# Sparse attention with a feed-forward layer on one core: a causal triangle added by TensorE in place of a select on GpSimd, and another order in the fourth slot

## The chip, the cores and the metric

The kernel runs on one core of a Trainium2 chip. A core has TensorE (PE: matmuls; PEld: its weight loads), VectorE (DVE), ScalarE (ACT), GpSimd (POOL) and SyncE (SP); DMA transfers are issued by SP, ACT and POOL. The metric is the time of one execution on the device in microseconds (us).

## The reference

Two stages follow each other: attention in which each query looks at the best six of 24 chunks of 32 keys, then a feed-forward layer with a squared ReLU.

```python
B, H, S, D = 4, 8, 768, 64          # chunk = 32, top_k = 6
ub = sum(maximum(q * k_min, q * k_max), -1)      # a bound for each query and chunk
ub = where(pos // 32 >= chunk_index, ub, -1e9)
top_chunks = argsort(ub)[..., -6:]
scores = q @ k.T / sqrt(D)
mask = (chunk of key in top_chunks) & (pos_q >= pos_k)
attn = softmax(where(mask, scores, -1e9))
x = (attn @ v)                       # heads side by side: (3072, 512)
out = maximum(x @ w_in, 0) ** 2 @ w_out          # w_in 512 x 2048, w_out 2048 x 512
```

Inputs and output are float32.

## The kernel before

The work is cut into eight half batches (one batch element, 384 of its 768 queries), in the order `ORDER`: first halves of batches 0 and 1, second halves of both, then batches 2 and 3. A half batch has four *slots*, each a pair of heads; there are 32 slots, and `NP` is 4. A first half sees only the keys of its own three tiles of 128.

The steps of a slot `s`:

- `step_T` transposes k and q of the two heads on TensorE (tiles `tk`, `tq`). ACT makes `qr`, the positive and the negative part of q (`relus_T`); DVE finds each chunk's minimum and maximum (`extrema`, L231, L234: `km`, `kbd`); `place` copies k and q into `kq`.
- `step_U` computes the bounds `ub` on TensorE (L372, L376), their eight largest on DVE (L390) and the choices (L392).
- `step_V` transposes the choices on TensorE (L425; L436 from slot 4 on) and copies them into `kq` (L430; L441), below q's 64 rows. There they meet rows that hold -2^24 at each chunk's keys, so that the score matmul itself takes chunks that are not chosen far down.
- `step_E(s, hh, n)` computes transposed scores of head `hh` (keys on partitions, queries along the columns), bank `n` of `BANKS`, on TensorE (L454, tile `ps`, three buffers), and their exponential on ACT (L460, tile `e`). In a first half, bank 0 holds key tile 0 against three query tiles and key tile 2 against one; bank 1 holds key tile 1 against two. After bank 1, one `affine_select` on POOL (L464) puts zeros above the diagonal of the three square tiles.
- `step_F` multiplies `e` with v (L482, tile `po`; a column of ones beside v gives the sum), divides (L491, L492) into `x`.

When a half batch is done, `x_T` transposes its x and `x_copy` moves it to `xT` (L520, L526), and `push` puts its feed-forward pieces into a queue: 16 `ffn_up` (L568, four matmuls each, then ReLU and square) and `ffn_down` (L591). They are taken from the queue one by one between the steps of later slots. `busy(n)` issues `n` dummy matmuls of ident with ident (L674) whose result nobody reads.

All is emitted in an order written out by hand: each engine takes its instructions in program order and waits on the semaphores of what it needs. The tiles `ub`, `qt`, `po` and `idle` (the dummies') share one pool of two buffers, `psA`, in order of their creation. The first four slots have the order of the loop at L708; from slot 4 on the loop at L750 holds. POOL's order in the first 30 us is: the identity, loads of k, q and v, and then, between the selects of slots 0 to 3, further loads (`later`, run by `go`): codes, w_in, v, k, q, w_out.

Of the kernel before, what the change touches and what calls it, by code (L numbers as in the profile page):

```python
# [9 lines left out]
BF16 = mybir.dt.bfloat16  # L10
AX = mybir.AxisListType
ALU = mybir.AluOpType
# [7 lines left out]
OFFSEL = -float(2 ** 24)  # L20


BANKS = (
# [3 lines left out]
)  # L27
# [12 lines left out]
def kernel(  # L40
# [61 lines left out]
    def load_packed(n, g, h0=0, h1=H):  # L102

        nc.gpsimd.dma_start(
            out=packed(n, g)[:, h0:h1],
            in_=rows(n, *ORDER[g], h0, h1).rearrange("h (p j) d -> p h (j d)", j=TP))
# [7 lines left out]
    def load_q0(h):  # L114
        nc.gpsimd.dma_start(
            out=qn0[:, :, h // 2, h % 2, 0:D],
            in_=q[0, h, 0:HB].rearrange("(j p) d -> p j d", p=128))
# [31 lines left out]
        nc.vector.memset(vn[i][:, :, :, D:D + 1], 1.0)  # L149
    ident = consts.tile([128, 128], BF16, tag="ident")  # L150
    make_identity(nc, ident)
    load_packed("k", 0, 4)
    for h in (4, 5):
        load_q0(h)
# [1 line left out]
        load_vt(0, j, 0, H // 2)  # L156
    for h in (6, 7):
        load_q0(h)
    for n in "kq":
        load_packed(n, 1)  # L160
    for j in range(HT):
# [61 lines left out]
    def extrema(s, part=None):  # L223
        b, half, p = slots[s]
        kv = st[s]["k"].rearrange("r (j c e) -> r c j e", j=TP, c=12)
        if part in (None, 0):
            st[s]["km"] = work.tile([128, 2, 12], BF16, tag="km", name="km")
        km = st[s]["km"]
        for w in range(2):
            if part in (None, w):  # L230
                nc.vector.tensor_reduce(km[:, w, :], kv, axis=AX.XY, op=(ALU.min, ALU.max)[w])  # L231
        if part in (0, 1):
            return
        nc.vector.tensor_mul(  # L234
            kbds[b % 2][:, p, :, :, 12 * half:12 * half + 12], hmask,
            km.unsqueeze(2).to_broadcast([128, 2, 2, 12]))
# [54 lines left out]
    def place(s, n, copy, h0=0, h1=2):  # L291
        b, half, p = slots[s]
        for h in range(h0, h1):
            copy(by_token(kqs[b % 2][0:D, p, 2 * half + "kq".index(n), h, :]),  # L294
                 in_order(st[s][n][D * h:D * h + D]))
# [67 lines left out]
    def step_U(s):  # L363
        b, half, p = slots[s]
        st[s]["e"] = [None, None]
        ncs = 12 * (half + 1)
        j0 = 1 - half
        nj = HT - j0
        bank = psA.tile([128, 192], F32, tag="att", name="ub")
        ub = bank[:, 0:2 * nj * ncs].rearrange("p (j h c) -> p j h c", j=nj, h=2)  # L370
        if not half:
            nc.tensor.matmul(  # L372
                bank[:, 0:48], lhsT=ident, rhs=cmask[:, 0:48], start=True, stop=False)
        for j in range(j0, HT):
            for w in range(2):
                nc.tensor.matmul(  # L376
                    ub[:, j - j0], lhsT=st[s]["qr"][:, w, 128 * j:128 * (j + 1)],
                    rhs=kbds[b % 2][:, p, w, :, 0:ncs],
                    start=bool(half) and j == 0 and w == 0,
                    stop=(not half and j == HT - 1 and w == 1))  # L380
        if half:
            diag = bank[:, 12:12 + HT * 52].rearrange("p (j x) -> p j x", j=HT)
            nc.tensor.matmul(  # L383
                diag[:, :, 0:48].rearrange("p j (h c) -> p j h c", h=2)[:, :, :, 0:4],
                lhsT=ident, rhs=cdiag[:, 0:1].to_broadcast([128, HT, 2, 4]),
                start=False, stop=True)
        m8 = work.tile([128, HT, 2, 8], F32, tag="m8", name="m8")
        for j in range(j0, HT):
            for hh in range(2):
                nc.vector.max(out=m8[:, j, hh, :],  # L390
                              in_=ub[:, j - j0, hh, 0:12 * half + 4 * j + 4])
        nc.vector.tensor_tensor(  # L392
            (qn0[:, j0:, p, :, D:D + ncs] if s < NP else
             chosen[s % 2][:, j0:, :, 0:ncs] if s < ON_PE * NP else
             nsel[half][:, s % 2, :, j0:, 1, 0:ncs].rearrange("p h j c -> p j h c")),
            ub, m8[:, j0:, :, TOPK - 1:TOPK].to_broadcast([128, HT - j0, 2, ncs]),
            op=ALU.is_lt)

    def qc(s, h):
        b, half, p = slots[s]  # L400
        return kqs[b % 2][0:KR, p, 2 * half + 1, h, :]
# [16 lines left out]
    def step_V(s):  # L418
        b, half, p = slots[s]
        if s < NP or s == ON_PE * NP:  # L420

            qt = psA.tile([128, 2, HB], BF16, tag="att", name="qt")
            for hh in range(2):
                for j in range(HT):
                    nc.tensor.matmul(  # L425
                        qt[0:KR, hh, 128 * j:128 * (j + 1)],
                        lhsT=qn0[:, j, p, hh, :] if s < NP else
                        nsel[half][:, s % 2, hh, j].rearrange("r n d -> r (n d)")[:, 0:KR],
                        rhs=ident, is_transpose=True, start=True, stop=True)
            nc.vector.tensor_copy(kqs[b % 2][0:KR, p, 2 * half + 1], qt[0:KR])  # L430
            return
        j0 = 1 - half
        c = 128 * j0
        qt = psA.tile([128, HB], BF16, tag="att", name="qt")
        for j in range(j0, HT):
            nc.tensor.matmul(  # L436
                qt[0:2 * CR, 128 * j:128 * (j + 1)],
                lhsT=chosen[s % 2][:, j].rearrange("r h c -> r (h c)"),
                rhs=ident, is_transpose=True, start=True, stop=True)
        for h in range(2):  # L440
            nc.vector.tensor_copy(  # L441
                kqs[b % 2][D:KR, p, 2 * half + 1, h, c:], qt[CR * h:CR * h + CR, c:])

    def step_E(s, hh, n):
        b, half, p = slots[s]
        t = st[s]
        if n == 0:
            t["e"][hh] = work.tile([128, 1920], BF16, tag="e", bufs=4, name="e")
        e = t["e"][hh]
        ps = psS.tile([128, 512], F32, tag="ps", name="ps")  # L450
        lo, hi = 512, 0
        for (at, j, i0, m) in BANKS[half][n]:
            c = 128 * (i0 - HT * half)
            nc.tensor.matmul(  # L454
                ps[:, at:at + 128 * m],
                lhsT=kqs[b % 2][0:KR, p, 2 * (j // HT), hh,
                                128 * (j % HT):128 * (j % HT + 1)],
                rhs=qc(s, hh)[:, c:c + 128 * m], start=True, stop=True)
            lo, hi = min(lo, at), max(hi, at + 128 * m)
        nc.scalar.activation(e[:, 512 * n + lo:512 * n + hi], ps[:, lo:hi], ACT.Exp,  # L460
                             scale=float(scale))
        if n == 1:
            d = e[:, 0:1152].rearrange("p (a c) -> p a c", a=3)[:, :, 0:128]
            nc.gpsimd.affine_select(  # L464
                out=d, in_=d, compare_op=ALU.is_ge, fill=0.0, base=0,
                channel_multiplier=-1, pattern=[[0, 3], [1, 128]])
# [203 lines left out]
    def busy(n, pool=psA, tag="att"):  # L670

        idle = pool.tile([128, 128], F32, tag=tag, name="idle")
        for _ in range(n):
            nc.tensor.matmul(idle, lhsT=ident, rhs=ident, start=True, stop=True)  # L674
# [32 lines left out]
    late = ctx.enter_context(tc.tile_pool(name="late", bufs=2))  # L707
    for s in range(NP):  # L708
        last = s + 1 == NP
        if s:  # L710
            step_E(s, 0, 0)
            if not last:

                step_T(s + 2, F, Y, "k")
                extrema(s + 2, 0)
            step_E(s, 0, 1)
        step_E(s, 1, 0)
        step_U(s + 1)
        busy(6)
        if not last:  # L720
            extrema(s + 2, 1)
            place(s + 1, "k", nc.scalar.copy)
        step_E(s, 1, 1)
        if last:
            x_T(0, 0, F)
            x_copy(0, 0, 0, 2, nc.scalar.copy)
            place(s + 1, "q", nc.scalar.copy)
            place(s + 1, "k", nc.scalar.copy, 1, 2)
        else:
            step_T(s + 2, F, Y, "q")  # L730
            relus_T(s + 2)
        step_V(s + 1)
        if s:
            step_F(s - 1, 0)
            step_F(s - 1, 1)
        if last:
            step_F(s, 0)
            step_F(s, 1)
        else:
            extrema(s + 2, 2)  # L740
            if s + 2 == NP:
                place(s + 2, "k", nc.vector.tensor_copy, 0, 1)
        go(s, 99)
# [181 lines left out]
```

## Time and profile before

| | |
|---|---|
| median of 3 runs | 267.62 us (267.55 to 269.31) |
| the profiled execution | 267.47 us |
| its span, from the first to the last instruction | 265.7 us |
| mean granted TensorE clock | 0.994 of full speed |
| busy: PE, ACT, DVE, POOL | 256.1, 178.0, 163.4, 94.5 us |

A row of the timeline has the start and the length in us, the engine, the line, the operation, out<-in, sizes, how many instructions of the kind were merged (x6), and in brackets how long the engine had been idle before it and what ended that. `idle` in a row's operands is the dummies' tile. A row of the table by stretches has for each engine the busy time and, in brackets, the number of instructions; then PEclk, the granted clock, the mean busy share of the DMA engines, and GB/s. A row of the chain has start, length and what was on the chain.

### The profile page before, as it was taken

To read this page: it belongs to the slowest core of one execution; us is meant where nothing else is said; L and a number is where in the kernel's file an instruction comes from. 1 tells how busy PE (TensorE), PEld (TensorE's weight loads), DVE (VectorE), ACT (ScalarE), POOL (GpSimd) and SP (SyncE) were. 2 spreads that over 40 slices of the span, in tenths; PEclk is the share of its full clock that TensorE was granted. 3 is DMA by queue.
4 is the path that set the end of the run, shared out by engine and by line. 5 is a ranking of instruction groups with operands and counts; after the bars stand their busy time and mean duration, and the time that the engine had idled before them with its cause. 6 is when DMAs were issued, how large, how long until landed. Compare 5 with 4: busy or idle time off the path is not lost.

```text
span 265.7 us, 6574 instructions
## 1 busy us (share of the span) xinstructions
PE 256.1 (96%) x2415; PEld 157.1 (59%) x2415; DVE 163.4 (61%) x618; ACT 178.0 (67%) x399; POOL 94.5 (36%) x141
## 2 busy tenths in 40 slices
PE   7887999999999999999999999999999999999995
PEld 6564566556656566655665566655565566745543
DVE  6895899776987468556875576555863233424421
ACT  5996798588976688845575787934685788614500
POOL 8998446515912425225611544221120111000000
PEclk9998899999999999999999999999999999999999
DMA  7999999999993799999996999996542220111022
GB/s 135 171 185 188 205 217 191 114 178 114 151 169 77 141 154 166 117 181 129 185 153 138 136 142 168 197 87 158 123 99 69 72 44 17 56 42 41 0 81 79
DMA packets 116161, 33.69 MB, mean 127 GB/s; under 512 B 102560, under 2 KB 112576, under 8 KB 116128
## 3 DMA queue, kind: packets, MB, share of 16 engines
q0 software_dynamic: 65200, 13.83, 64.3%
q1 hardware_dynamic: 49984, 19.03, 38.6%
q10 hardware_dynamic: 944, 0.39, 0.6%
q8 instruction: 19, 0.31, 0.5%
q14 instruction: 14, 0.11, 0.1%
HBM read 27.26 MB, written 6.29 MB: 126 GB/s over the span
## 4 chain that ended last, share of the span: by engine, by line
PE 78%; DVE 8%; POOL 5%; ACT 3%; DMA 2%; issue 2%; DVEq 0%; POOLq 0%; ACTq 0%
PE py L591 29%; PE ph L568 27%; PE ps L454 11%; PE po L482 7%; DMA kn<-in_k_dram 2%; DVE km L337 2%; POOL vn L125 2%; POOL e L464 2%; PE ub L376 1%; ACT e L460 1%; PE py L556 1%; DVE km L231 1%; DVE kq L441 1%; DVE h L579 1%; DVE kq L294 1%
## 5 line engine op out<-in xcount | busy, mean ns | idle before, releaser
L460 ACT ACTIVATE e<-ps 128x512 bf16<-128x512 f32 x192 | 96.4, 550 | 19.5 <-PE ps L454 19.2
L568 PE MATMUL ph<-xT,w_in 128*128 128x384 bf16 x512 | 100.1, 328 | 0.1
L591 PE MATMUL py<-w_out,h 128*128 128x512 bf16 x368 | 88.1, 379 | 0.5 <-DVE kq L294 0.3
L464 POOL TENSOR_SCALAR_AFFINE_SELECT e<-e 128x384 bf16<-128x384 bf16 x64 | 34.2, 540 | 131.2 <-ACT e L460 130.3
L579 DVE TENSOR_TENSOR h<-ht 128x384 bf16<-128x384 bf16 x114 | 41.8, 376 | 55.6 <-ACT ht L578 55.0
L578 ACT ACTIVATE ht<-ph 128x384 bf16<-128x384 f32 x114 | 55.5, 500 | 27.0 <-PE ph L568 26.5
L568 PEld LDWEIGHTS <-w_in 128*128 128x128 bf16 x512 | 48.2, 98 | 31.1 <-issue 2.2
L454 PE MATMUL ps<-kq 96*128 96x384 bf16 (+2 forms) x320 | 57.6, 278 | 1.3 <-DVE kq L430 0.9
L591 PEld LDWEIGHTS <-h 128*128 128x128 bf16 x368 | 34.6, 97 | 35.6 <-issue 0.6
L454 PEld LDWEIGHTS <-kq 96*128 96x128 bf16 x320 | 26.4, 97 | 16.2 <-issue 1.7
L482 PEld LDWEIGHTS <-e 128*128 128x128 bf16 x672 | 25.3, 98 | 6.0 <-POOL e L464 2.3
L482 PE MATMUL po<-vn,e 128*128 128x65 bf16 x672 | 27.0, 194 | 1.8 <-POOL e L464 1.5
L597 ACT COPY ob<-py 128x512 f32<-128x512 f32 x18 | 10.6, 586 | 22.6 <-PE py L591 22.3
L390 DVE MAX8 m<-ub 128x8 f32<-128x16 f32 (+4 forms) x160 | 16.1, 166 | 15.4 <-PE ub L383 9.3
L492 DVE TENSOR_TENSOR x<-po,r 128x384 bf16<-128x384 f32 x32 | 17.8, 557 | 1.1
L109 POOL DMA_DIRECT2D kn<-in_k_dram x15 | 13.3, 892 | 0.4 <-issue 0.3
L109 POOL DMA_DIRECT2D qn<-in_q_dram x15 | 13.3, 893 | 0.2
L231 DVE TENSOR_REDUCE km<-tk 128x12 bf16<-128x384 bf16 x24 | 12.5, 551 | 0.9 <-PE tk L268 0.7
L125 POOL DMA_DIRECT2D vn<-in_v_dram x15 | 12.5, 841 | 0.7 <-issue 0.6
L337 DVE TENSOR_TENSOR km<-km 128x384 bf16<-128x384 bf16 (+3 forms) x40 | 11.7, 294 | 1.1
L376 PEld LDWEIGHTS <-qr 128*128 128x128 bf16 x160 | 7.9, 96 | 5.3 <-DVE qr L317 1.7
L376 PE MATMUL ub<-kbd,qr 128*128 128x48 bf16 (+1 forms) x160 | 9.7, 180 | 1.3 <-DVE kbd L234 0.5
(75 smaller groups left out, 188.5 us busy)
## 6 DMA issues: line engine op xcount, KB each, us to landing
out_dram<-ob SPq DMA_DIRECT2D x23, 256.0 KB, 2.7
w_out<-in_moe_w_out_dram POOLq DMA_DIRECT2D x2, 1024.0 KB, 16.8
kn<-in_k_dram POOLq DMA_DIRECT2D x15, 128.0 KB, 5.6
qn<-in_q_dram POOLq DMA_DIRECT2D x15, 128.0 KB, 5.5
kq<-kqT SPq DMA_DIRECT2D x10, 192.0 KB, 4.8
vn<-in_v_dram POOLq DMA_DIRECT2D x4, 384.0 KB, 8.2
vn<-in_v_dram POOLq DMA_DIRECT2D x9, 128.0 KB, 8.1
w_in<-in_moe_w_in_dram POOLq DMA_DIRECT2D x2, 512.0 KB, 8.0
```

The lines of the kernel that those rows point to most:

```text
L109: nc.gpsimd.dma_start(out=nat_of(n, g)[:, DM * j:DM * j + DM].rearrange("p (h d) -> p h d", d=D), in_=rows(n, *ORDER[g], 0, H)[:, 128 * j: ...
L125: nc.gpsimd.dma_start(out=vn[b % 2][:, h0:h1, j, 0:D], in_=v[b, h0:h1, 128 * j:128 * (j + 1)].rearrange("h p d -> p h d"))
L376: nc.tensor.matmul(ub[:, j - j0], lhsT=st[s]["qr"][:, w, 128 * j:128 * (j + 1)], rhs=kbds[b % 2][:, p, w, :, 0:ncs], start=bool(half) and ...
L454: nc.tensor.matmul(ps[:, at:at + 128 * m], lhsT=kqs[b % 2][0:KR, p, 2 * (j // HT), hh, 128 * (j % HT):128 * (j % HT + 1)], rhs=qc(s, hh)[: ...
L460: nc.scalar.activation(e[:, 512 * n + lo:512 * n + hi], ps[:, lo:hi], ACT.Exp, scale=float(scale))
L464: nc.gpsimd.affine_select(out=d, in_=d, compare_op=ALU.is_ge, fill=0.0, base=0, channel_multiplier=-1, pattern=[[0, 3], [1, 128]])
L482: nc.tensor.matmul(po[:, hh, i, :], lhsT=t["e"][hh][:, c:c + 128], rhs=vn[b % 2][:, 2 * p + hh, j, :], start=(j == 0), stop=(j == iq))
L492: nc.vector.tensor_mul(x[:, p].rearrange("p j (h d) -> p h j d", h=2), po[:, :, :, 0:D], r.to_broadcast([128, 2, HT, D]))
L568: nc.tensor.matmul(ph[:, 0:HB], lhsT=w_in[:, ki, 128 * f:128 * (f + 1)], rhs=xT[:, ki, :], start=(ki == 0), stop=(ki == NKI - 1))
L578: nc.scalar.activation(ht, ph[:, 0:HB], ACT.Relu)
L579: nc.vector.tensor_mul(h, ht, ht)
L591: nc.tensor.matmul(py[t], lhsT=h2[hb, f][:, 128 * t:128 * (t + 1)], rhs=w_out[:, f, :], start=(f == 0), stop=(f == NFI - 1))
```

## The change

1. A constant `tri` of 128 x 128 is made at the start: DVE fills it with -2^24, and POOL, after the loads of q for heads 6 and 7, keeps that where the partition is greater than the column and puts zeros elsewhere.
2. In slots 0 to 3, `step_E` adds `tri` to each square tile on the diagonal with a matmul (weights `ident`, 128 columns) behind the scores, in the same bank: two in bank 0 and one in bank 1. The `affine_select` is left out there, and stays for slot 4 and later.
3. In slots 0 to 2 there are three dummies behind the bounds in place of six. In slot 3 the six are left out, and four stand ahead of its scores.
4. In slot 3, slot 2's products (`step_F(s - 1)`) move ahead of slot 4's bounds (`step_U`), and slot 4's choices (`step_V`) move behind slot 3's own products.

```diff
     ident = consts.tile([128, 128], BF16, tag="ident")
     make_identity(nc, ident)
+
+    tri = consts.tile([128, 128], BF16, tag="tri", name="tri")
+    nc.vector.memset(tri, OFFSEL)
     load_packed("k", 0, 4)
...
     for h in (6, 7):
         load_q0(h)
+    nc.gpsimd.affine_select(
+        out=tri, in_=tri, compare_op=ALU.is_ge, fill=0.0, base=-1,
+        channel_multiplier=1, pattern=[[-1, 128]])
     for n in "kq":
         load_packed(n, 1)
...
-                rhs=qc(s, hh)[:, c:c + 128 * m], start=True, stop=True)
+                rhs=qc(s, hh)[:, c:c + 128 * m], start=s >= NP or lo == 512, stop=s >= NP)
             lo, hi = min(lo, at), max(hi, at + 128 * m)
+        if s < NP:
+            for (at, j, i0, m) in BANKS[half][n]:
+                nc.tensor.matmul(
+                    ps[:, at:at + 128], lhsT=ident, rhs=tri, start=False,
+                    stop=at == BANKS[half][n][-1][0])
         nc.scalar.activation(e[:, 512 * n + lo:512 * n + hi], ps[:, lo:hi], ACT.Exp,
                              scale=float(scale))
-        if n == 1:
+        if n == 1 and s >= NP:
             d = e[:, 0:1152].rearrange("p (a c) -> p a c", a=3)[:, :, 0:128]
             nc.gpsimd.affine_select(
...
     for s in range(NP):
         last = s + 1 == NP
+        if last:
+            busy(4)
         if s:
             step_E(s, 0, 0)
...
             step_E(s, 0, 1)
         step_E(s, 1, 0)
+        if last:
+            step_F(s - 1, 0)
+            step_F(s - 1, 1)
         step_U(s + 1)
-        busy(6)
         if not last:
+            busy(3)
             extrema(s + 2, 1)
             place(s + 1, "k", nc.scalar.copy)
         step_E(s, 1, 1)
...
             place(s + 1, "q", nc.scalar.copy)
             place(s + 1, "k", nc.scalar.copy, 1, 2)
+            step_F(s, 0)
+            step_F(s, 1)
+            step_V(s + 1)
         else:
             step_T(s + 2, F, Y, "q")
             relus_T(s + 2)
-        step_V(s + 1)
-        if s:
-            step_F(s - 1, 0)
-            step_F(s - 1, 1)
-        if last:
-            step_F(s, 0)
-            step_F(s, 1)
-        else:
+            step_V(s + 1)
+            if s:
+                step_F(s - 1, 0)
+                step_F(s - 1, 1)
             extrema(s + 2, 2)
```

## The prediction

> **What bounds the kernel now.** I read the page first, then the chain of waits, then the timeline up to 30 us, then the busy times stretch by stretch.
>
> ```profile
> span 265.7 us, 6574 instructions
> PE 256.1 (96%) x2415; PEld 157.1 (59%) x2415; DVE 163.4 (61%) x618; ACT 178.0 (67%) x399; POOL 94.5 (36%) x141
> PE   7887999999999999999999999999999999999995
> PEclk9998899999999999999999999999999999999999
> ```
>
> TensorE is busy nearly all the time except in the first four slices of 6.64 us, and these are what the change edits. From the fifth slice on the order on TensorE is full, so what the head gains should reach the end, and nothing more. The two 8s in the clock row (19.9 to 33.2 us) are the other thing to explain. The head ends like this:
>
> ```profile
> 20.77 0.58 DVE L441 COPY kq<-qt 32x256 bf16<-32x256 bf16 x2 [0.39 <-PE qt L436]
> 21.74 0.20 DVE L491 RECIPROCAL r<-po 128x6 f32<-128x6 f32 x1 [0.39 <-PE po L482]
> 21.97 0.56 DVE L492 TENSOR_TENSOR x<-po,r 128x384 bf16<-128x384 f32 x1
> 22.55 1.03 POOL L464 TENSOR_SCALAR_AFFINE_SELECT e<-e 128x384 bf16<-128x384 bf16 x2
> 23.17 0.83 PE L482 MATMUL po<-vn,e 128*128 128x65 bf16 x12 [1.47 <-POOL e L464]
> 23.84 0.38 PE L454 MATMUL ps<-kq 96*128 96x384 bf16 x2
> 24.67 0.82 PE L520 MATMUL pt<-ident,x 128*128 128x128 bf16 x6
> 25.59 0.56 DVE L526 COPY xT<-pt 128x768 bf16<-128x768 bf16 x1 [0.76 <-PE pt L520]
> 26.20 1.98 PE ph L568 x6
> 28.26 1.46 PE L568 MATMUL ph<-xT,w_in 128*128 128x384 bf16 x8
> 28.41 1.31 PE ph L568 x8
> ```
>
> Slot 3's products (L482 at 23.17) wait 1.47 us for slot 3's causal select, because POOL runs it in its queue behind DMA issues. Then follow x, its transposes (24.67), their copy (25.59), and the feed-forward matmuls (26.20). These take 1.98 / 6 = 0.33 us each, and 1.31 / 8 = 0.163 after 28.41. The next table says why:
>
> ```profile
> core 0: us, PE busy (x) PEld busy (x) DVE busy (x) ACT busy (x) POOL busy (x), PEclk, DMA share, GB/s
> 10.88:14.30 3.42, 2.77 (x42) 1.97 (x39) 2.58 (x11) 3.29 (x9) 3.42 (x7) 1.00 1.42 190
> 17.71:21.12 3.41, 2.81 (x46) 2.15 (x43) 2.83 (x13) 3.34 (x9) 3.41 (x6) 1.00 1.23 194
> 21.12:24.54 3.42, 1.74 (x40) 1.18 (x36) 1.45 (x5) 1.63 (x5) 3.42 (x7) 1.00 1.90 171
> 24.54:27.96 3.42, 3.35 (x22) 1.79 (x17) 2.61 (x7) 2.24 (x6) 1.90 (x3) 0.50 1.37 208
> ```
>
> The granted clock is 0.50 from 24.54 to 27.96, straight after the one stretch of that length in which TensorE was busy 1.74 us; stretches with 2.77 and more are followed by 1.00. So the wait for POOL costs once by itself and perhaps once more through the clock.
>
> **The change, part by part.** Each slot of the first four repeats one closed loop, here slot 1 to slot 2:
>
> ```profile
> 12.21 0.38 PE L454 MATMUL ps<-kq 96*128 96x384 bf16 x2 [0.65 <-DVE kq L430]
> 13.18 0.25 PE L376 MATMUL ub<-kbd,qr 128*128 128x24 bf16 x4
> 13.28 0.49 PE L674 MATMUL idle<-ident 128*128 128x128 bf16 x6
> 13.47 0.40 DVE L390 MAX8 m<-ub 128x8 f32<-128x8 f32 x4
> 13.91 0.21 DVE L392 TENSOR_TENSOR qn<-ub,m 128x48 bf16<-128x48 f32 x1
> 14.48 0.54 PE L482 MATMUL po<-vn,e 128*128 128x65 bf16 x12
> 14.69 0.55 DVE L430 COPY kq<-qt 96x768 bf16<-96x768 bf16 x1
> 15.29 0.38 PE L454 MATMUL ps<-kq 96*128 96x384 bf16 x2 [0.27 <-ACT e L460]
> ```
>
> Scores, bounds, the eight largest, choices, their transposes, the copy into kq, next scores: 15.29 - 12.21 = 3.08 us, each step starting within 0.1 us of the one before it.
>
> *Triangles.* 24 matmuls of 128 columns with ident as weights, which is also what a dummy is.
>
> ```profile
> L674 PE MATMUL idle<-ident x75: 216/219/314, 1.4 to 19.8; 128*128 128x128 bf16 x75
> L674 PEld LDWEIGHTS <-ident x75: 95/98/151, 1.4 to 19.7; 128*128 128x128 bf16 x75
> ```
>
> Six dummies take 0.49 us, the last of them 0.219 from start to end, so one step is (0.49 - 0.22) / 5 = 0.055 us. No row shows a triangle behind a score matmul. The lower bound is 0.055; the upper is a weight load that nothing hides, at worst 0.151. I take 0.055, since weights and columns are the same. Five of a slot's six triangles stand ahead of its bounds, so each loop becomes 5 x 0.055 = 0.28 longer. The sixth, and the removed dummies, stand behind the bounds, where TensorE waits for L392 anyway: three dummies fewer gain nothing, and are costed at nothing.
>
> Two loops have slack:
>
> ```profile
> 10.04 0.14 PEld L376 LDWEIGHTS <-qr 128*128 128x128 bf16 x3 [0.18 <-ACT qr L289]
> 16.24 0.19 PE L372 MATMUL ub<-cmask,ident 128*128 128x48 bf16 x1
> 16.36 0.25 PE L376 MATMUL ub<-kbd,qr 128*128 128x24 bf16 x4
> ```
>
> In slot 0 the bounds wait 0.18 for ACT's qr, which stands behind the first exponential; only the two triangles ahead of that one count, 0.11. In slot 2 they start 0.12 after L372 instead of the 0.03 that slot 1 shows, and L390 is some 0.05 late: 0.28 - 0.12 = 0.16. Sum at slot 3: 0.11 + 0.28 + 0.16 = 0.55.
>
> *Four dummies ahead of slot 3.* Their tile takes the buffer of slot 3's qt (two buffers, and po came between), so they wait for the copy L430 and stand ahead of the scores that wait for the same copy: 4 x 0.055 = 0.22 on the path.
>
> ```profile
> 18.50 0.71 PE L454 MATMUL ps<-kq 96*128 96x384 bf16 x5 [0.27 <-DVE kq L430]
> 18.98 1.64 ACT L460 ACTIVATE e<-ps 128x512 bf16<-128x512 f32 x4
> 19.04 0.19 PE L372 MATMUL ub<-cmask,ident 128*128 128x48 bf16 x1
> 19.97 0.50 PE L520 MATMUL pt<-ident,x 128*128 128x128 bf16 x6
> ```
>
> Slot 3's scores start at 18.50 + 0.55 + 0.22 = 19.27.
>
> *Slot 3's new order.* Three score groups: 0.54 us of steps (18.50 to 19.04, where the bounds came) and five triangles, 0.28: 20.09. Slot 2's products, whose exponentials are long done: 0.54, to 20.63. Reciprocal and x: 0.04 + 0.79 (21.74 to 22.53) = 21.46. L390 and L392 queue behind that on DVE; before, the bounds came first. Slot 3's products need the buffer of slot 2's po, free at 21.46; the four exponentials (1.64 from 19.8) end about then too: 21.51 to 22.05 instead of 24.00. Reciprocal and x again: 22.88. The choices' copies (two in 0.58) now come behind x, the first done at 23.20. Slot 4's scores start at 23.25 instead of 23.84: **0.59 earlier**. So of 1.95 us won at the products, 1.36 go to the late choices. Scores to the second x transposes as before (24.67 - 23.84 = 0.83): 24.08; at full clock 0.50: 24.58; copy, with its 0.04 ahead: 25.18; feed-forward at 25.23 instead of 26.20: **0.97 earlier**.
>
> *The clock.* If it halves again from 24.54 to 27.96: six matmuls at 0.33 to 27.21, then slot 4's second group and bounds, 0.24 at full clock (28.02 to 28.26) and about 0.4 at half, so the next feed-forward matmul starts near 27.6. By 27.96 it has done 0.18 us of full-speed work; before, the same one started at 28.26. The gain is 28.26 - (27.96 - 0.18) = **0.48 us**. If it stays open: 25.23 + 6 x 0.163 + 0.24 = 26.45, a gain of **1.8**.
>
> Which? By the forecast times TensorE is busy in 21.12 to 24.54 for 0.15 (end of the first x transposes), 0.54, 0.30 (choices' transposes) and 1.29, in all 2.3 us: halfway between 1.74 and 2.77. Most of what is added there is transposes of tk, tq, x and choices; ordinary matmuls are 12 products and two scores, as before. I go with halving, since the ordinary matmuls are no more than in the stretch that was followed by 0.50.
> The Trainium skill ("TensorE: Matmul & The Clock Gate", Part 4, PE-mode transpose) says that transposes don't count as TensorE activity as other matmuls do; by that the stretch is as empty as before and the time is the first of the two. The trace can't separate them.
>
> *The rest.* POOL loses eight selects of about 0.52; its DMA issues come up to 4.2 us earlier. None of TensorE's waits in the rows above, or elsewhere up to 30 us, is for a DMA, so that is worth nothing. No moved step issues a DMA, so the SP and POOL queues change no order. The triangle's own select is as long as the identity's:
>
> ```profile
> 1.08 0.29 POOL masks.py:199 TENSOR_SCALAR_AFFINE_SELECT ident<-ident 128x128 bf16<-128x128 bf16 x1
> 8.09 0.83 POOL L104 DMA_DIRECT2D kn<-in_k_dram  x1 [0.49 <-DMA kn<-in_k_dram]
> 6.25 0.14 PEld L376 LDWEIGHTS <-qr 128*128 128x128 bf16 x3 [0.16 <-ACT qr L289]
> ```
>
> It fits into the 0.49 that POOL waits for a DMA; without that cover it would delay loads by 0.29 us. Its memset on DVE, about 0.1, is hidden in slot 0's 0.16 wait for ACT; without it, it would be 0.1 on the path.
>
> **Sum.** Profiled execution 267.47 (span 265.7 and 1.77 around it); the median of the runs is 267.62, 0.15 above. 267.62 - 0.48 = **267.1**. Its own range, for triangles up to 0.07 and a clock that halves a little later: 266.6 to 267.5.
>
> **Rivals.**
> *The clock stays open.* For: the longest idle stretch of TensorE shrinks from 1.47 to about 0.9, and 2.3 us lie nearer to 2.77 than 1.74 does. Against: the stretch is filled with transposes. 267.62 - 1.8 = 265.8; if the loops also cost less, 265.3.
> *The triangles cost a whole weight load.* Seventeen of them stand on the path (2, 5, 5 and 5). At 0.151 they add 17 x 0.096 = 1.63 to slot 4's start; the first 0.36 of it costs half, since it falls in half-clock time: 0.18 + 1.27 = 1.45, so the change loses 0.97, **268.6**, slower. It decides from 0.66 us of extra, 0.094 a triangle, just under the 0.098 of one load. Against: the ident load ahead of L372 stands behind a score matmul too, and the three score groups with it run without a gap.
> The same page (Back-to-back issue gap) gives about 81 ns for a 128-column matmul with its load in a stream; by that the gain would be 0.22, 267.4, but the dummies here step at 0.055.
> *The change moves the wait only.* If slot 4's scores wait for something else until 23.84, such as the copies of q on ACT, which follow the x copy there, nothing is won: 267.6.
>
> **How the numbers follow.** The forecast has 0.52, the open clock 0.27, the dear triangles 0.11, the moved wait 0.10. The range is 265.5 to 268.2: it takes in the forecast, most of the open clock, the moved wait and the cheaper half of the dear triangles. A measurement here can tell about 1% (2.7 us) from no change. Only an open clock together with shorter loops reaches 264.9: 0.05. Slower than 270.3 needs dear triangles and another halved stretch: 0.03.
>
> **What would show it.** Right: no wait of L482 for POOL; scores of slots 1, 2 and 3 start 0.11, 0.39 and 0.77 later; slot 4's at 23.25; feed-forward past its copy at 25.2; 0.50 in the clock from 24.54. Wrong: triangles stepping at 0.1 or more, a clock of 1.00 throughout, a second halved stretch because there are fewer dummies, or TensorE waiting for DMA before 45 us.

## The result and the profile after

The change made the kernel a little faster: a median of 266.30 us (22 runs, 265.88 to 267.59) against 267.59 (22 runs, 266.03 to 269.47). The ratio is 0.9955, with a 95% interval of 0.9933 to 0.9976: some 1.2 us, where 0.48 was forecast. The interval leaves out 1, but a difference of under 1% counts as the same here. The profiled execution took 266.18 us, with a span of 264.5.

The page of the kernel after, the lines that answer to those of before:

```profile
span 264.5 us, 6559 instructions
PE 253.7 (96%) x2402; PEld 157.4 (60%) x2428; DVE 162.5 (61%) x619; ACT 178.4 (67%) x399; POOL 91.1 (34%) x134
PE   7897999999999999999999999999999999999995
PEclk9999999999999999999999999999999999999999
```

The two 8s in the clock row are gone. The new lines are L460 for the scores, L468 triangles, L471 exponentials, L493 products, L503 x, L436 and L447 copies into kq, L531 and L537 the x transposes and their copy, and L579 feed-forward. The timeline of the kernel after:

```profile
8.78 0.38 PE L460 MATMUL ps<-kq 96*128 96x384 bf16 x2 [0.34 <-DVE kq L436]
12.68 0.38 PE L460 MATMUL ps<-kq 96*128 96x384 bf16 x2 [0.65 <-DVE kq L436]
12.89 0.28 PE L468 MATMUL ps<-tri,ident 128*128 128x128 bf16 x2
16.05 0.38 PE L460 MATMUL ps<-kq 96*128 96x384 bf16 x2 [0.27 <-DVE kq L436]
19.42 0.38 PE L685 MATMUL idle<-ident 128*128 128x128 bf16 x4 [0.27 <-DVE kq L436]
19.64 0.39 PE L460 MATMUL ps<-kq 96*128 96x384 bf16 x2
21.89 0.55 PE L493 MATMUL po<-vn,e 128*128 128x65 bf16 x12 [0.25 <-DVE x L503]
22.71 0.56 DVE L503 TENSOR_TENSOR x<-po,r 128x384 bf16<-128x384 f32 x1
23.29 0.60 DVE L447 COPY kq<-qt 32x256 bf16<-32x256 bf16 x2
23.72 0.38 PE L460 MATMUL ps<-kq 96*128 96x384 bf16 x2 [0.98 <-DVE kq L447]
25.12 0.56 DVE L537 COPY xT<-pt 128x768 bf16<-128x768 bf16 x1 [1.23 <-ACT qr L295]
25.73 1.14 PE L579 MATMUL ph<-xT,w_in 128*128 128x384 bf16 x6 [0.38 <-DVE xT L537]
26.98 0.81 PE L579 MATMUL ph<-xT,w_in 128*128 128x384 bf16 x4
```

Slot 3's products (21.89) no longer wait for POOL but for the x whose buffer they take. The choices' copies (23.29) stand behind the second x (22.71), and slot 4's scores wait 0.98 us for them. The feed-forward's six matmuls take 1.14 and not 1.98: they run at the full clock, and the seventh starts at 26.98 in place of 28.26.

This execution reached its first scores at 8.78, against 8.42 in the one of before. Experiment 11 comes back to that; distances below are taken from the first scores or from slot 1's where that matters, and before rounding, so they can differ by 0.01 from the rows.

### The profile page after: what moved, and what is told of

It is laid out like the page before. It is cut to its first block, busy times and chain, and to the rows that moved or that the text cites. A ratio compares the mean times of both kernels' runs of the same rounds, so it can differ in the third digit from the quotient of the medians.

```text
span 264.5 us, 6559 instructions
## 1 busy us (share of the span) xinstructions
PE 253.7 (96%) x2402; PEld 157.4 (60%) x2428; DVE 162.5 (61%) x619; ACT 178.4 (67%) x399; POOL 91.1 (34%) x134
## 4 chain that ended last, share of the span: by engine, by line
PE 77%; DVE 8%; ACT 3%; issue 2%; ACTq 0%; DVEq 0%
PE py L602 28%; PE ph L579 26%; PE ps L460 11%; PE po L493 7%; DVE km L343 2%; ACT e L471 2%; PE ub L382 1%; PE py L567 1%; DVE km L237 1%; DVE kq L447 1%; DVE h L590 1%; DVE kq L300 1%; ACT ht L589 1%; PE tk L274 0%; ACT ob L608 0%
## 5 line engine op out<-in xcount | busy, mean ns | idle before, releaser
L471 ACT ACTIVATE e<-ps 128x512 bf16<-128x512 f32 x192 | 96.7, 550 | 18.9 <-PE ps L460 17.6
L579 PE MATMUL ph<-xT,w_in 128*128 128x384 bf16 x512 | 98.9, 325 | 0.4 <-DVE xT L537 0.4
L602 PE MATMUL py<-w_out,h 128*128 128x512 bf16 x342 | 82.7, 379 | 2.2 <-DVE kq L300 0.3
L475 POOL TENSOR_SCALAR_AFFINE_SELECT e<-e 128x384 bf16<-128x384 bf16 x56 | 30.1, 537 | 129.0 <-ACT e L471 128.8
L579 PEld LDWEIGHTS <-w_in 128*128 128x128 bf16 x512 | 47.8, 97 | 30.7 <-issue 1.5
L460 PE MATMUL ps<-kq 96*128 96x384 bf16 (+2 forms) x320 | 57.9, 278 | 2.2 <-DVE kq L436 1.3
L460 PEld LDWEIGHTS <-kq 96*128 96x128 bf16 x320 | 26.4, 97 | 17.0 <-issue 2.6
L493 PEld LDWEIGHTS <-e 128*128 128x128 bf16 x672 | 25.2, 98 | 4.1 <-DVE x L503 0.4
L493 PE MATMUL po<-vn,e 128*128 128x65 bf16 x672 | 26.6, 194 | 0.3 <-DVE x L503 0.3
L503 DVE TENSOR_TENSOR x<-po,r 128x384 bf16<-128x384 f32 x32 | 17.8, 557 | 1.1
```

The lines of the kernel that those rows point to most:

```text
L460: nc.tensor.matmul(ps[:, at:at + 128 * m], lhsT=kqs[b % 2][0:KR, p, 2 * (j // HT), hh, 128 * (j % HT):128 * (j % HT + 1)], rhs=qc(s, hh)[: ...
L475: nc.gpsimd.affine_select(out=d, in_=d, compare_op=ALU.is_ge, fill=0.0, base=0, channel_multiplier=-1, pattern=[[0, 3], [1, 128]])
L493: nc.tensor.matmul(po[:, hh, i, :], lhsT=t["e"][hh][:, c:c + 128], rhs=vn[b % 2][:, 2 * p + hh, j, :], start=(j == 0), stop=(j == iq))
L503: nc.vector.tensor_mul(x[:, p].rearrange("p j (h d) -> p h j d", h=2), po[:, :, :, 0:D], r.to_broadcast([128, 2, HT, D]))
L579: nc.tensor.matmul(ph[:, 0:HB], lhsT=w_in[:, ki, 128 * f:128 * (f + 1)], rhs=xT[:, ki, :], start=(ki == 0), stop=(ki == NKI - 1))
L602: nc.tensor.matmul(py[t], lhsT=h2[hb, f][:, 128 * t:128 * (t + 1)], rhs=w_out[:, f, :], start=(f == 0), stop=(f == NFI - 1))
```

## The experiments

Each was timed in turns with the kernel before, in one of three sessions on three chips. Medians of before there were 267.68 (experiments 1, 2, 3 and 5), 267.63 (4, 6, 8 and 9) and 268.06 (7, 10 and 12). The whole change was not timed again in them, so a few tenths between an experiment's median and its 266.30 are no proof by themselves; the distances in the traces are given beside them.

**1. Triangles alone**, old order, six dummies.

```diff
  (from the whole change)
         if last:
-            busy(4)
...  the loop over slots 0 to 3 as in the kernel before
```

> The kernel before with the triangle matmuls in place of the select in slots 0 to 3, but the old order and the six dummies in each slot. Theory (the whole gain is the removed wait for POOL, by itself and through the clock, and the new order of slot 3 gives part of it back by its late choices): slot 3's scores 0.55 later than before, the products of slots 2 and 3 without a wait for POOL, slot 4's scores near 22.0 instead of 23.84 and feed-forward matmuls past their copy near 24.2 in place of 26.20, 1 us ahead of the whole change; ratio to before 0.989 to 0.993 (264.7 to 265.7). Rival (the order is needed, the triangles alone only move the wait): no gain over before or less than the whole change, 266.5 to 267.6.

Measured: 265.55 us, ratio 0.9913 (0.9886 to 0.9940), better than the whole change. The timeline of this kernel:

```profile
12.80 0.38 PE L460 MATMUL ps<-kq 96*128 96x384 bf16 x2 [0.65 <-DVE kq L436]
21.51 0.30 PE L442 MATMUL qt<-ident,chosen 128*64 128x128 bf16 x2
21.74 0.55 PE L493 MATMUL po<-vn,e 128*128 128x65 bf16 x12
22.48 0.55 PE L493 MATMUL po<-vn,e 128*128 128x65 bf16 x12 [0.19 <-DVE kq L447]
22.93 0.38 PE L460 MATMUL ps<-kq 96*128 96x384 bf16 x2
25.04 1.14 PE L579 MATMUL ph<-xT,w_in 128*128 128x384 bf16 x6 [0.34 <-DVE xT L537]
```

With the choices' transposes first (21.51), slot 4's scores follow the last products without a wait. From slot 1's first scores (12.80 here) to slot 4's it is 10.13 us, against 11.05 in the whole change and 11.63 in the first profile of before. So the triangles alone win 1.50 there, and the new order with its dummies gives 0.92 of that back. The scores came at 22.93 and not at 22.0; 0.48 of that is this execution's later start (8.90 against 8.42).

**2. The order alone**, with the select on POOL.

```diff
  (from the kernel before)
+        if last:
+            busy(4)
...  the loop over slots 0 to 3 as in the whole change, no triangles
```

> The kernel before with the new order of the fourth slot and the new dummies (three, and four ahead of slot 3), but with the select on POOL. Theory: slot 2's products stand ahead of slot 4's bounds and wait for POOL there (20.9 in the trace of before), so bounds, choices and slot 3's second exponentials all wait with them: slot 4's scores 1.0 to 1.5 later than before, 268.5 to 269.0. Rival (the order carries the gain): 266.3 to 267.0.

Measured: 269.89 us, ratio 1.0080 (1.0051 to 1.0109): slower, and by more than expected. Timeline and stretches of this kernel:

```profile
21.25 0.83 PE L482 MATMUL po<-vn,e 128*128 128x65 bf16 x12 [1.39 <-POOL e L464]
23.56 0.98 PE L482 MATMUL po<-vn,e 128*128 128x65 bf16 x12 [0.85 <-POOL e L464]
25.82 0.48 PE L454 MATMUL ps<-kq 96*128 96x384 bf16 x1 [0.94 <-DVE kq L441]
```

```profile
19.07:22.48 3.41, 1.91 (x33) 1.42 (x31) 1.41 (x5) 1.68 (x5) 3.41 (x6) 1.00 1.30 200
22.48:25.90 3.42, 1.63 (x19) 1.00 (x17) 2.17 (x10) 2.28 (x5) 3.09 (x6) 0.50 2.05 175
25.90:29.31 3.41, 3.35 (x29) 1.94 (x29) 1.36 (x4) 2.08 (x5) 1.26 (x2) 0.50 1.14 211
```

Both pairs of products wait for POOL, 1.39 and 0.85 us, slot 4's scores come at 25.82 (23.84 before), and the clock is halved for two stretches in a row. The expectation had the waits and left out the second halving. The new order needs the triangles; the triangles do not need it.

**3. Activity in the wait**, the kernel before with 24 dummies ahead of slot 3's products, and **4. the same with transposes**.

```diff
         if last:
+            busy(24)          # 3; in 4: 24 matmuls of ident, is_transpose=True
             step_F(s, 0)
             step_F(s, 1)
```

> The kernel before with 24 more dummies (1.3 us) ahead of slot 3's products, where TensorE waited 1.47 us for POOL: the wait stays, only the activity of TensorE differs. Theory (the wait costs a second time through the clock): granted clock 1.00 behind the wait, feed-forward matmuls at 0.163 instead of 0.33, 0.8 us faster where the clock had been halved: median 266.5 to 267.0. Rival (the half clock costs nothing, other waits hide it): 267.6.

> The kernel before with 24 transposes of ident, not dummies, ahead of slot 3's products, where TensorE waited for POOL. If transposes count as activity for the clock: as with the dummies there, clock 1.00 and a median near 266.7. If they do not: the clock is halved as in the kernel before, median 267.6. Theory, weakly: they count, since the clock stayed open in the whole change, whose added activity there is mostly transposes.

Measured: 266.72 us (ratio 0.9965, 0.9947 to 0.9984) with dummies, 266.78 (0.9973, 0.9945 to 1.0001) with transposes. First the rows with dummies, then those with transposes:

```profile
23.39 0.56 PE L482 MATMUL po<-vn,e 128*128 128x65 bf16 x12
20.01:23.42 3.41, 3.18 (x57) 2.80 (x56) 2.29 (x10) 3.14 (x8) 3.41 (x8) 1.00 1.50 193
23.42:26.83 3.41, 3.16 (x47) 2.03 (x45) 2.29 (x6) 2.40 (x6) 2.24 (x5) 1.00 1.82 185
```

```profile
19.83:23.25 3.42, 3.19 (x57) 2.82 (x57) 2.27 (x10) 3.25 (x8) 3.42 (x7) 1.00 1.46 193
23.25:26.66 3.41, 3.06 (x46) 1.96 (x44) 2.19 (x5) 2.27 (x6) 2.21 (x4) 1.00 1.86 183
```

The products still come as late as POOL lets them (23.39, before 23.17), and yet the kernel gains 0.96 us. That is the clock alone: in the same session, five of the 24 runs of before had a mean clock of 1.00, and they took 266.35 to 266.99 without any dummies. Transposes hold the clock as dummies do: the mean clock was 0.999 or more in 12 of 12 runs with dummies and in 11 of 12 with transposes (0.987 in the other), against 5 of 24 and 9 of 35 runs of before beside them. The interval of 4 just touches 1; the open clock in its profile (1.00 after 23.25) is plain. The Trainium skill's remark that transposes don't count like other matmuls ("TensorE: Matmul & The Clock Gate", Part 4) does not hold for this stretch.

**5. Without the four dummies** ahead of slot 3's scores.

```diff
-        if last:
-            busy(4)
```

> The whole change without the four dummies ahead of slot 3's scores. Theory (they stand on the path, 0.22): slot 3's scores and all behind them 0.22 earlier than in the whole change, 266.0 to 266.2. Rival (they keep the clock open, and without them it is halved more often): 266.5 or more.

Measured: 266.07 us, 0.23 under the whole change; from slot 1's first scores to slot 3's 6.75 us against 6.96. The 0.22 of the prediction is there. Three of twelve runs lay at 267.4 to 267.6, with a mean clock of 0.994, as five of 22 of the whole change did at 267.2 to 267.6, so there is no sign that the four dummies served the clock.

**6. Choices first**: only `step_V` moved back ahead of slot 3's products.

```diff
+            step_V(s + 1)
             step_F(s, 0)
             step_F(s, 1)
-            step_V(s + 1)
```

> The whole change with one move undone: in slot 3 the choices' transposes (step_V) stand ahead of slot 3's products again; bounds stay behind slot 2's products. Theory (late choices give back part of the gain: their copies wait behind the second x on DVE): slot 4's scores 0.4 earlier than in the whole change, feed-forward 0.4 to 0.6 earlier, 265.7 to 265.9. Rival (the products' x ahead of the choices is what gains): 0.3 us or more slower than the whole change, 266.6 or more.

Measured: 265.86 us (ratio 0.9919, 0.9892 to 0.9946), within the expected range. Slot 1's first scores and slot 4's:

```profile
12.62 0.38 PE L460 MATMUL ps<-kq 96*128 96x384 bf16 x2 [0.64 <-DVE kq L436]
23.16 0.38 PE L460 MATMUL ps<-kq 96*128 96x384 bf16 x2
```

Between them are 10.53 us against 11.05. Choices behind the second x cost about half a microsecond.

**7. Bounds first**: only `step_U` moved back ahead of slot 2's products.

```diff
+        step_U(s + 1)
         if last:
             step_F(s - 1, 0)
             step_F(s - 1, 1)
-        step_U(s + 1)
```

> The whole change with slot 4's bounds ahead of slot 2's products again; the choices' transposes stay behind slot 3's products. Theory (on DVE the eight largest and the choices now stand ahead of slot 2's x, whose buffer slot 3's products need, and nothing uses the earlier choices): 0.2 to 0.4 slower than the whole change, 266.5 to 266.7. Rival (late bounds are what gives the gain back): 0.3 faster, 266.0.

Measured: 266.00 us (ratio 0.9927, 0.9903 to 0.9951), where slower than the whole change was expected. Against the 17 runs of the whole change with a mean clock of 0.999 or more (median 266.26) it is 0.26 faster, but the two sets overlap, so that is not clear of the noise. In the traces, slot 4's scores come 0.21 earlier behind the first ones (14.74 against 14.94). The rival's size fits; its timeline shows why:

```profile
21.45 0.21 DVE L398 TENSOR_TENSOR chosen<-ub,m 128x48 bf16<-128x48 f32 x1
21.72 0.74 PE L493 MATMUL po<-vn,e 128*128 128x65 bf16 x12
21.80 0.56 DVE L503 TENSOR_TENSOR x<-po,r 128x384 bf16<-128x384 f32 x1
```

The products at 21.72 start before slot 2's x (21.80) has even begun. In this order the shared pool hands them the buffer of the bounds, free after the choices at 21.45 + 0.21, and not that of slot 2's po. My expectation had kept the buffers of the other order.

**8. Six dummies in slots 0 to 2.**

```diff
-            busy(3)
+            busy(6)
```

> The whole change with six dummies in slots 0 to 2 in place of three. Theory (dummies behind the bounds hide in TensorE's wait for the choices): the same time as the whole change within 0.2, scores of slots 1 to 3 at the same distances. Rival (they are on the path at 0.055 each): 3 x 3 x 0.055 = 0.5 us slower, 266.8.

Measured: 266.70 us, nearer to the rival's 266.8. In the trace slot 1's first scores to slot 4's took 11.13 us against 11.05: 0.09 for six dummies more, where 0.33 would stand on the path. They are mostly hidden. The profiled execution (266.73) began late by as much as it is slower: its first scores came at 9.20 in place of 8.78, and nothing ahead of them was edited. Whether the median of twelve runs is high by such chance as well is open.

**9. The remaining idle time filled**: 16 dummies behind the choices' transposes.

```diff
             step_V(s + 1)
+            busy(16, psS, "ps")
```

> The whole change with 16 more dummies (0.9 us) behind the choices' transposes in slot 3, where TensorE still idles about 1.1 us. Theory (the runs of the whole change at 267.2 to 267.6, with a clock of 0.994, are halved windows that fall on this idle stretch): those runs vanish, the rest stay at 266.0 to 266.5. Rival (they come from something else): one run in four or five still at 267.2 or more.

Measured: 266.31 us; the highest of twelve runs is 266.65. The whole change had five of 22 at 267.17 to 267.59, each with a mean clock of 0.994, the other 17 at 0.999 or 1.000. That fits the theory; 0 of 12 after 5 of 22 could also be luck, though not often.

**10. Triangles doubled.**

```diff
             for (at, j, i0, m) in BANKS[half][n]:
-                nc.tensor.matmul(
+                for r in range(2):
+                    nc.tensor.matmul(
```

> The whole change with each triangle added twice (24 more matmuls). Theory (17 of 24 triangles stand on the path to slot 4's scores at 0.055 to 0.06 each): the distance from slot 1's first scores to slot 4's grows by 15 x 0.056 = 0.84, time 267.1 to 267.3. Rival (they hide in waits for DVE and ACT): under 0.3 more, 266.3 to 266.6. Rival (each costs a weight load, 0.1): 1.5 more, 267.8.

Measured: 267.44 us, 1.14 over the whole change, 0.14 above the expected range; four of twelve runs had a mean clock of 0.994, and the other eight a median of 267.29. From slot 1's first scores (12.86) to slot 4's (24.76) 11.90 us against 11.05: 0.85 longer, where 0.84 was expected. A triangle is on the path and costs 0.056 there.

**11. The kernel before, profiled again.**

> The kernel before, one more profile. Theory (the stretches of 3.41 us over which the clock is decided start at another moment in each execution): the full clock begins at another time than 4.07, the halved stretch, if there is one, lies a whole number of 3.41 us behind that, and the time differs by up to 1.5 us. Rival (the stretches start with the program): the same 4.07 and 24.54 again.

Measured: 267.61 us. Dummies, scores and products of that execution, then its stretches:

```profile
5.90 1.25 PE L674 MATMUL idle<-ident 128*128 128x128 bf16 x10
9.20 0.38 PE L454 MATMUL ps<-kq 96*128 96x384 bf16 x2 [0.34 <-DVE kq L430]
23.38 0.83 PE L482 MATMUL po<-vn,e 128*128 128x65 bf16 x12 [1.40 <-POOL e L464]
24.05 0.48 PE L454 MATMUL ps<-kq 96*128 96x384 bf16 x1
20.69:24.10 3.41, 1.90 (x36) 1.41 (x34) 1.75 (x8) 2.69 (x7) 3.41 (x7) 1.00 1.57 188
24.10:27.51 3.41, 3.35 (x33) 1.94 (x30) 1.99 (x5) 2.08 (x5) 2.17 (x4) 0.50 1.73 189
```

The halved stretch lies at 24.10 and not at 24.54. The ten dummies ahead of the first bounds, 0.73 us in the first profile, took 1.25 here, about 0.1 each: the full clock began, by the trace's record, at 7.03 and not at 4.07. From there to the halved stretch are 17.07 us, five stretches of 3.41; in the first profile 20.48, six. The grid of stretches starts at another place in each execution. In the fourteen profiles of all these kernels the first scores come the later, the later the full clock begins: from 8.42 where it began at 4.07 to 9.20 where it began at 7.03.

One more thing is to be read here. The first scores come 0.78 later than in the first profile (9.20 for 8.42), slot 4's scores only 0.21 (24.05 for 23.84): POOL's queue sets the products' time, and takes up a late start (its last select ahead of them starts at 22.74, in the first profile at 22.55).

**12. A version built from these**: triangles, bounds first, slot 2's products in the wait for the choices, three and no dummies.

```diff
  (from experiment 1)
-        busy(6)
         if not last:
+            busy(3)
...
         if last:
+            step_F(s - 1, 0)
+            step_F(s - 1, 1)
             x_T(0, 0, F)
...
-        if s:
+        if s and not last:
             step_F(s - 1, 0)
```

> Triangles as in the change; in slot 3 the bounds first, then slot 3's last scores, slot 2's products, the first x transposes, the choices' transposes, slot 3's products; three dummies in slots 0 to 2 and none in slot 3. Theory: slot 2's products fill TensorE's wait for the choices, whose copies no longer stand behind the second x; slot 4's scores some 0.2 earlier than with triangles alone in the old order, 265.2 to 265.5. Rival (ACT's four exponentials and the x copy set the pace there): 265.5 to 265.7, no gain over the triangles alone.

Measured: 265.73 us (ratio 0.9912, 0.9880 to 0.9944), no better than the triangles alone at 265.55 (from slot 1's first scores to slot 4's 10.27 us, there 10.13). The trace names the next wait:

```profile
22.25 0.97 ACT L300 COPY kq<-tq 64x384 bf16<-64x384 bf16 x2
22.77 0.38 PE L460 MATMUL ps<-kq 96*128 96x384 bf16 x2 [0.16 <-ACT kq L300]
```

Slot 4's scores wait for ACT's copies of q, which follow the x copy and the exponentials there: the rival's pace.

## Why the prediction was right or wrong

*The time.* 267.1 was forecast, 266.3 measured: inside the range, on the right side, the gain too small by more than half. The range covered both states of the clock, so being inside it does not show that the clock was read rightly.

*The loops: right.* Against the first scores of each execution, slots 1, 2 and 3 begin 0.11, 0.40 and 0.78 later than before (forecast 0.11, 0.39, 0.77). Experiments 5 and 10 confirm two terms by themselves: the four dummies 0.21, a triangle 0.056. The dear triangles are out. The triangle's own select on POOL took 0.47 us and not the identity's 0.29; it still cost nothing, since POOL waited another 0.34 for a DMA behind it.

*POOL's wait goes and the order gives it back: right in the main.* The products at 21.89 and the copies behind x at 23.29 stand as forecast. Against the first scores, slot 4's came 14.94 us later, 15.42 in the first profile of before: 0.48 won, forecast 0.59; the feed-forward past its copy came 0.83 earlier, forecast 0.97. But that profile was a lucky one to win against. In the second profile of before (experiment 11) the same distance is 14.85, since POOL takes up a late start and the loop of the kernel after does not; there the change wins nothing at this point. And the sum took the new order as given. Experiment 1 shows that it cost time, and experiment 6 that the choices' move took about half a microsecond of it (0.44 by the medians); for the bounds' move experiment 7 has 0.21 in the traces and 0.30 by the medians, which is not clear of the noise.

*The clock: the step that failed.* "I go with halving, since the ordinary matmuls are no more than in the stretch that was followed by 0.50." The clock stayed open in the profile and in 16 other runs of 22. The stretches of the kernel after:

```profile
19.15:22.57 3.42, 2.90 (x53) 2.44 (x52) 2.79 (x13) 3.14 (x9) 3.34 (x5) 1.00 1.35 201
22.57:25.98 3.41, 2.05 (x30) 1.28 (x30) 2.08 (x6) 2.96 (x8) 1.44 (x3) 1.00 2.04 178
25.98:29.39 3.41, 3.41 (x28) 2.02 (x26) 3.31 (x14) 2.86 (x8) 1.46 (x3) 1.00 1.13 212
```

Two things were wrong. Transposes count (experiment 4), so the ordinary matmuls were the wrong measure. And I read the grid of one execution as the program's own. Here the idle time falls into a stretch with 2.05 us of TensorE, and that was enough. It is also the least that this trace holds in any 3.41 us behind the first scores, wherever the grid lies; the two traces of before go down to 1.59 and 1.90. All the runs bear this out: where the emptiest such stretch of a kernel's trace has 2.34 or more (experiments 1, 3, 4, 6, 9 and 12), one run of 61 had a mean clock below 0.999; at 2.00 to 2.05 (the whole change, 5, 7, 8 and 10) 14 of 69; and of the kernel before 65 of 82 in the three sessions. The rival of the open clock should have had the larger chance; its 1.8 would have been 1.28 between these two profiles (28.26 to 26.98).

*Where the gain came from.* Activity alone, with POOL's wait left in place, brings 0.96 us (experiment 3). Wait, triangles, dummies and new order together add only the remaining 0.4 (266.72 to 266.30). So most of what this change won was the half clock behind POOL's wait. That the wait itself brought so little is the doing of the new order and its dummies: the triangles alone, timed in the same session as experiment 3, take another 1.17 us off (266.72 to 265.55), with the clock open in both.

## What to carry to other kernels

A wait on TensorE can cost twice, once while it lasts and once through the clock of the stretch after it. Filling the wait with dummies or transposes wins back the second part alone (here 0.96 us); taking the wait away wins both (2.1). When a change has several parts, run each alone: here the mask on TensorE was worth 2.1 us by itself, and the order and dummies shipped with it took 0.8 of that back. If a reordered step shares a small pool of buffers, work out again which buffer each tile gets.

## What the runs showed of the hardware

The clock is decided in stretches of 3.41 us, and the grid shifts from one execution to the next. The full clock began at 4.07 and 7.03 us in two profiles of one kernel, and the first scores moved from 8.42 to 9.20 with it. A single profile shows one draw: the runs of before scatter over 3.4 us (266.03 to 269.47), while the six of experiment 1, all with the clock open, stay within 0.4.

By the profile's busy time, stretches with 1.74, 1.90 and 1.91 us of TensorE were followed by the half clock, and one with 2.05 was not. In these profiles the line lies between 1.91 and 2.05, with transposes counted in. That 14 of 69 runs were halved in the kernels whose emptiest stretch had 2.00 to 2.05 suggests that it lies close to those; no profile of such a run was kept.
